# Attention and FFN block on one core: separate dependency records for four slices, product order at the end of a burst, 16-bit tile ends moved into the query groups, paired reciprocals

## The chip, the cores and the metric

The kernel runs on one core of one Trainium2 chip. The metric is the device time of one execution in microseconds (us); less is better. Different submissions ran on different chips, and the unchanged kernel's median moved between 577.3 and 581.1 us with them, so kernels are compared by their ratio to the kernel before, run alternately with it on the same chip. A ratio is the mean time of one kernel's fast runs over the mean of the other's in the same rounds, so it is not quite the ratio of the medians quoted beside it.

Engines: PE is the tensor engine, DVE the vector engine, ACT the scalar engine, POOL and SP issue the DMAs (POOL also computes a few small values at the start).

## The reference, cut to what matters

```python
xn = layernorm(x)                        # x: 1 x 2048 x 448, bf16
q = (xn @ wq) in 16 heads of 256         # 8 key/value heads, window of 512 keys
p = softmax(q k^T / 16);  o = p @ v
s = o @ wo                               # 4096 -> 448
g = silu((gelu(xn @ w_gate) * (xn @ w_up)) @ w_down)
return x + s * g
```

The kernel computes g first, stores it (g2) in device memory, and then goes through four chunks of 512 queries with 16 heads each. For the first three chunks, `o @ wo` is done in one go after the chunk's last head, by a scheme of eight products on sums of halves (a "burst"). Its result is folded, transposed by DMA into `sT`, and combined with x and g in four "tile ends", one for each 128 rows.

## The kernel before

Dependencies come from buffer records: an operation waits for the last writer of what it reads, and for the last writer and all readers of what it writes. The record, not the address, decides.

```python
def op(self, eng, fn, reads=(), writes=(), dma=False, after=()):
    raw = {b.writer: None for b in reads if b.writer is not None}
    deps = dict(raw)
    for b in writes:
        if b.writer is not None:
            deps[b.writer] = None
        deps.update((x, None) for x in b.readers)
    # ... (an engine doesn't wait for itself, except for what it reads)
```

The end of a burst. Note `bx`: one list of records for all four slices `xs[0..3]`.

```python
xs = [xnT[:, k, 0:QC] for k in range(4)]
bx = [y for t in range(4) for y in b_xnT[t]]
def part(eng, b, V, bV, r, n, slot):      # half to xs[n], half to cc, then swap partitions on ACT
    for o, bo, lo, hi in ((xs[n][:, r*HC:r*HC+HC], bx, 0, HC),
                          (cc[:, slot, 0, :], b_cc[slot][:1], HC, QC)):
        # ... ACT copy, or DVE add of V
    act(cc[own, slot, 1, :], cc[other, slot, 0, :], ACT.Copy, ...)
def fold(r, n, slot):
    add("dve", xs[2][own, ...], cc[own, slot, 0, :], cc[own, slot, 1, :], b_cc[slot], bx)
# product 0, product N, product 1, the products on sums (6, 5, 4, 2), product 3; then
add("dve", U2, bank[B6], U2, ...); add("dve", U3, bank[B7], U2, ...)
part("dve", B5, U3, b_tmp[1], 1, 1, 3)
add("dve", U2, bank[B5], U2, ...)
part("dve", B3, U2, b_tmp[0], 0, 1, 0)
dma_t(sT[:, :, 1, :], xs[1], bx, (b_sT[1],))
part("dve", B1, U3, b_tmp[1], 1, 0, 1)
dma_t(sT[:, :, 0, :], xs[0], bx, (b_sT[0],))
for r, n, slot in ((0, 0, 2), (1, 1, 3), (0, 1, 0), (1, 0, 1)):
    fold(r, n, slot)
dma_t(sT[:, :, 2, :], xs[2], bx, (b_sT[2],))
```

After a burst come four query groups (two heads' q each; the results are cast to qT, half on ACT and half on DVE), then heads. A head `m` is: scores of four tiles, exponential with row sum on ACT, reciprocal and scaling on DVE, a DMA transpose of every two tiles into pT, and `p @ v` of head `m - 2`.

```python
for m in range(NS):
    if m in groups:
        for i in range(m, next_group, 2):
            q_group(i, ...)
    s_mm(m)
    if len(late) == LAG:            # LAG = 2
        pv(late.pop(0))
    if m > Hq and LAG <= m % Hq < LAG + 4:
        burst_end(m // Hq - 1, m % Hq - LAG)     # one tile end in each of four heads
    if m > Hq and m % Hq == LAG - 1:
        burst(m // Hq - 1)          # the last burst also issues the loads of wo, 4 x 0.9 MB
    late.append(m)

def wo_end(t, c0, c1, src):         # a tile end: three f32 multiplies by g2, one addition of x
    # ... DVE: tmp = src * f * g2;  xr = tmp + xr
    load_g2(t + NG2)                                      # POOL queue, NG2 = 2
    dma("pool", out_view[:, t, c0:c1], xr[:, x, c0:c1])   # POOL queue
    dma("pool", xr[:, x, :], x_view[:, t + NXR, :])       # POOL queue, NXR = 3; waits for the line above
```

The softmax here doesn't subtract the row's maximum and nothing guards it: scores larger than these inputs give would overflow.

## Time and profile before

| | before |
|---|---|
| time, median of its first three runs | 580.89 us |
| span of the profiled execution | 577.2 us |
| PE busy | 547.1 us, 95% |
| DVE busy | 371.9 us, 64% |
| query groups after burst 1, 2, 3 | 14.44, 16.79, 22.83 us (each read 0.23 us too long, see below) |
| PE waits in the heads that follow | 3.35, 3.2, 1.7 us |

The stretches are differences of times in the timeline of PE: from the first matmul on wq after a burst to the first score matmul after that. PE is the bound, so only the time in which it waits, or runs at a low clock, can be gained. Some records of matmuls are missing from a trace: this one holds x4419 matmuls. One of the missing is the first score matmul after each set of query groups (7 matmuls stand there beside 8 weight loads, of which the first starts 0.23 us before the first recorded matmul). So in traces with x4419 the query groups read 0.23 us too long and the heads after them 0.23 us too short. The page gives busy time as us (share) x instructions.

```profile
span 577.2 us, 11576 instructions
PE 547.1 (95%) x4419; PEld 288.0 (50%) x4444; DVE 371.9 (64%) x944; ACT 297.9 (52%) x771; POOL 44.6 (8%) x83
```

The list of waits of PE names two large causes: casts of qT, and transposes of pT (the numbers are us in all, how often, and the longest).

```profile
PE bank L366 <- DVE qT L701: 13.4, 4, 8.7
PE bank L366 <- DMA pT<-pn: 8.7, 7, 2.1
```

The timeline of PE shows where the first of them falls: the first matmuls of the third of the four query groups (columns: start, duration, engine, line, operation, operands, shape, count, and the idle time before it).

```profile
252.55 0.82 PE L366 MATMUL bank<-xnT,wq 64*128 64x512 bf16 x6 [1.84 <-DVE qT L701]
361.53 1.46 PE L366 MATMUL bank<-xnT,wq 64*128 64x512 bf16 x6 [2.74 <-DVE qT L701]
477.41 1.46 PE L366 MATMUL bank<-xnT,wq 64*128 64x512 bf16 x6 [8.69 <-DVE qT L701]
```

The second and third of these blocks take 1.46 us instead of 0.82: the granted clock, as the trace records it, had fallen to half. A cast lasts 0.7 us and cannot by itself hold PE for 8.69 us. The chain of waits, read in order of time in the third burst, shows what the cast had to wait for.

```profile
464.94 10.09 DMA sT<-xnT
475.13 0.13 DVE xnT L360
...
475.56 0.76 DVE xnT L360 x2
476.33 0.42 DVE xnT L360
476.75 0.61 DVE qT L701
...
477.41 7.78 PE bank L366 x56
```

The four folds (DVE xnT L360) write `xs[2]`. The transpose reads `xs[0]`. They share no byte, only the record `bx`; so DVE stood still for a DMA, and the casts behind the folds stood still too.

The second cause lies in the four heads that hold a tile end. These are one tile end's operations in the timeline of DVE, and one of the PE waits that follow.

```profile
263.17 0.62 DVE L755 SCALAR_TENSOR_TENSOR tmp<-sT,g 128x256 f32<-128x256 bf16 x2
263.70 0.22 DVE L755 SCALAR_TENSOR_TENSOR tmp<-sN,g 128x64 f32<-128x64 bf16 x1
263.95 0.62 DVE L360 TENSOR_TENSOR xr<-tmp,xr 128x448 bf16<-128x448 f32 x1
```

```profile
277.15 1.90 PE L366 MATMUL bank<-pT,va 128*128 128x512 bf16 x8 [1.99 <-DMA pT<-pn]
```

With the tile end, DVE needs about 4.3 us for such a head, and PE 3.45 us.

### The profile page before, as it was taken

What the parts mean: (1) busy time and instruction counts of PE and PEld (TensorE: products, weight loads), DVE (VectorE), ACT (ScalarE), POOL (GpSimd) and SP (SyncE); (2) the same over time, 40 slices, a digit from 0 to 9 for tenths busy, and PEclk for the clock granted to TensorE, in tenths of its full rate; (3) what the DMA queues carried; (4) which work ended last, traced back from release to release, by engine and by line L of the source; (5) the groups of instructions that cost most, each with busy time, mean ns of one, the idle gap of its engine ahead of it and who ended that gap; (6) DMA issues with size and microseconds to landing.
All of it is one profiled execution on the core that took longest, in us unless ns stands there. A gap on an engine that the chain in (4) does not pass through costs nothing.

```text
span 577.2 us, 11576 instructions
## 1 busy us (share of the span) xinstructions
PE 547.1 (95%) x4419; PEld 288.0 (50%) x4444; DVE 371.9 (64%) x944; ACT 297.9 (52%) x771; POOL 44.6 (8%) x83
## 2 busy tenths in 40 slices
PE   9999999999999999989799998989999949889998
PEld 5554444445444447934344496333447923334455
DVE  6665545753668589459858863697589516976822
ACT  5434447643568484137748712467585124676700
POOL 1140500000000000003100000030000010400000
PEclk9999999999999999999999999899999998999999
DMA  9565599722327365017925911199175171982601
GB/s 292 127 192 109 116 281 256 110 53 70 89 65 141 88 111 115 4 26 137 197 56 119 147 34 20 40 184 175 26 147 120 39 242 30 195 173 53 149 18 57
DMA packets 177767, 66.46 MB, mean 115 GB/s; under 512 B 159856, under 2 KB 173680, under 8 KB 177712
## 3 DMA queue, kind: packets, MB, share of 16 engines
q1 hardware_dynamic: 172960, 52.76, 43.7%
q0 software_dynamic: 3984, 12.39, 7.6%
q8 instruction: 35, 0.57, 0.4%
q10 hardware_dynamic: 768, 0.57, 0.3%
q14 instruction: 20, 0.16, 0.1%
HBM read 23.43 MB, written 3.67 MB: 47 GB/s over the span
## 4 chain that ended last, share of the span: by engine, by line
PE 76%; DMA 10%; DVE 10%; issue 3%; ACT 1%; DVEq 0%; ACTq 0%
PE bank L366 75%; DMA pT<-pn 7%; DMA sT<-xnT 3%; DVE pn L718 3%; DVE tmp L755 1%; DVE rden L717 1%; DVE oTh L738 1%; DVE xnT L360 1%; PE bank L483 1%; DVE tmp L360 1%; ACT qT L357 1%; ACT p L714 0%; DVE qT L701 0%; DVE xr L360 0%; DVE oT L738 0%
## 5 line engine op out<-in xcount | busy, mean ns | idle before, releaser
L714 ACT ACTIVATE p<-bank 128x512 f32<-128x512 f32 x256 | 149.9, 598 | 39.6 <-PE bank L366 19.9
L718 DVE TENSOR_SCALAR pn<-p,rden 128x512 bf16<-128x512 f32 x256 | 124.6, 487 | 18.3 <-DMA pT<-pn 9.5
L366 PE MATMUL bank<-pT,va 128*128 128x512 bf16 x512 | 120.9, 379 | 8.8 <-DMA pT<-pn 8.7
L366 PE MATMUL bank<-kT,qT 128*128 128x512 bf16 x487 | 118.2, 379 | 3.1 <-ACT qT L357 1.4
L366 PE MATMUL bank<-xnT,wq 64*128 64x512 bf16 x768 | 98.0, 384 | 14.0 <-DVE qT L701 13.3
L366 PEld LDWEIGHTS bank<-pT,va 128*128 128x128 bf16 x512 | 49.3, 98 | 71.7 <-DMA pT<-pn 13.7
L366 PE MATMUL bank<-xnT,wgu 64*128 64x512 bf16 (+2 forms) x768 | 83.9, 350 | 0.2
L366 PEld LDWEIGHTS bank<-kT,qT 128*128 128x128 bf16 x512 | 49.2, 98 | 63.4 <-issue 3.4
L357 ACT ACTIVATE qT<-bank 128x512 bf16<-128x512 f32 x64 | 37.8, 595 | 71.6 <-PE bank L366 70.2
L701 DVE CAST qT<-bank 128x512 bf16<-128x512 f32 x64 | 42.2, 688 | 42.4 <-PE bank L366 42.3
L366 PEld LDWEIGHTS bank<-xnT,wq 64*128 64x128 bf16 x768 | 36.9, 95 | 63.0 <-DVE qT L701 15.3
L366 PEld LDWEIGHTS bank<-xnT,wgu 64*128 64x128 bf16 x768 | 37.0, 94 | 37.1 <-issue 0.7
L532 DVE TENSOR_TENSOR actT<-bank,gl 128x512 bf16<-128x512 f32 x56 | 37.8, 690 | 26.5 <-PE bank L366 19.9
L714 ACT ACTIVATION_READ_ACCUMULATOR p<-bank 128x1 f32 x256 | 52.8, 206 | 0.0
L357 ACT ACTIVATE gl<-bank 128x512 bf16<-128x512 f32 x56 | 33.2, 597 | 37.0 <-PE bank L366 34.9
L717 DVE RECIPROCAL rden<-rsum 128x1 f32<-128x1 f32 x256 | 40.1, 157 | 15.9 <-ACT p L714 15.9
L366 PE MATMUL bank<-wd,actT 128*128 128x448 bf16 x224 | 43.0, 353 | 0.0
L351 POOL DMA_DIRECT2D g<-g_all x16 | 8.8, 552 | 369.1 <-DVE tmp L755 368.9
L738 DVE TENSOR_SCALAR oTh<-bank 128x512 f16<-128x512 f32 x48 | 32.8, 684 | 0.0
L366 PEld LDWEIGHTS bank<-wd,actT 128*128 128x128 bf16 x224 | 21.8, 98 | 21.0 <-issue 0.4
L366 PE MATMUL bank<-sr,wt 128*64 128x256 f16 x576 | 31.9, 273 | 0.0
L366 PEld LDWEIGHTS bank<-sr,wt 128*64 128x64 f16 x576 | 31.5, 110 | 0.0
(62 smaller groups left out, 423.8 us busy)
## 6 DMA issues: line engine op xcount, KB each, us to landing
wo<-in_A_wo_dram POOLq DMA_DIRECT2D x4, 896.0 KB, 7.1
wtb<-in_A_wo_dram POOLq DMA_DIRECT2D x4, 768.0 KB, 7.3
wq<-in_A_wq_dram SPq DMA_DIRECT2D x2, 1536.0 KB, 11.6
va<-in_A_v_cache_dram SPq DMA_DIRECT2D x8, 256.0 KB, 5.0
pT<-pn SPq DMA_TRANSPOSE x128, 2.8
g_all<-g2w SPq DMA_DIRECT2D x16, 112.0 KB, 1.9
xr<-in_A_x_dram POOLq DMA_DIRECT2D x16, 112.0 KB, 3.5
g<-g_all POOLq DMA_DIRECT2D x16, 112.0 KB, 2.7
```

The lines of the kernel that those rows point to most:

```text
L351: K.op(q, lambda e, o=o, i=i: e.dma_start(o, i), reads, writes, dma=True)
L357: K.op("act", lambda e, o=o, i=i: e.activation(o, i, func, scale=scale), reads, writes)
L360: K.op(eng, lambda e: e.tensor_tensor(o, x, y, op), reads, writes)
L366: ins = e.matmul(o, lhsT=l, rhs=r, start=st, stop=sp, skip_group_check=True)
L483: ins = e.matmul(bank[b][:, 0:w], lhsT=gl[:, 0, 0:P], rhs=gl[:, 0, 0:w], start=True, stop=True)
L532: K.op("dve", lambda e: e.tensor_tensor(actT[:, c % 2, f, :], bank[b + 1], gl[:, s, :], ALU.mult), (b_ps[b + 1], b_gl[s]), (b_actT[c % 2][ ...
L701: K.op("dve", lambda v, s=s, b=b: v.tensor_copy(qT[:, s, 1, :], bank[b + 1]), (b_ps[b + 1],), (b_qT[s][1],))
L714: K.op("act", lambda e, b=b, r=r, z=z: e.activation(p32[:, z, :], bank[b], ACT.Exp, scale=att_scale, accum_out=rsum[:, r:r + 1]), (b_ps[b] ...
L717: K.op("dve", lambda e, r=r: e.reciprocal(rden[:, r:r + 1], rsum[:, r:r + 1]), (b_rsum[r],), (b_rden[r],))
L718: K.op("dve", lambda e, r=r, z=z, y=y, t=t4 % 2: e.tensor_scalar(pn[:, y, t, :], p32[:, z, :], rden[:, r:r + 1], None, op0=ALU.mult), (b_p ...
L738: K.op("dve", lambda v, i=i, b=b, o=o, f=f: v.tensor_scalar(o[:, i, :], bank[b], f, None, op0=ALU.mult), (b_ps[b],), (b_oT[i],))
L755: K.op("dve", lambda e, at=at, i=i, f=f: e.scalar_tensor_tensor(out=at(tmp[:, s, :]), in0=i, scalar=f, in1=at(g2[:, g, :]), op0=ALU.mult, ...
```

## The change

The intent: the DVE sums and the first folds hide behind the last two products; the folds no longer wait for the transposes; the tile ends leave the heads for the query groups and become cheaper (16-bit multiplies; their constant factor `0.5 / (WS * WS)` moves into the sums at the end of the burst); DVE saves half of the reciprocals. The diff, cut to its core:

```diff
+        tmpb, _, _ = place("tmpb", [P, 2, 2 * QC], BF16, at=a)
+        b_xs = [K.buf() for k in range(4)]
...
-        def q_group(n, pairs):
+        def q_group(n, pairs, more_act=False):
+                if more_act and i:
+                    act(qT[:, s, 1, :], bank[b + 1], ACT.Copy, ...)      # third of four casts on ACT
+                    continue
...
-                K.op("dve", ... e.reciprocal(rden[:, r:r + 1], rsum[:, r:r + 1]) ...)
-                K.op("dve", ... tensor_scalar(pn[:, y, t, :], p32[:, z, :], rden[:, r:r + 1] ...) ...)
                 if t4 % 2 == 1:
+                    K.op("dve", ... e.reciprocal(rden[:, r - 1:r + 1], rsum[:, r - 1:r + 1]) ...)
+                    for t in range(2):
+                        K.op("dve", ... tensor_scalar(pn[:, y, t, :], ...) ...)
...
-                add("dve", xs[2][own, ...], ..., b_cc[slot], bx)
+                add("dve", xs[2][own, ...], ..., b_cc[slot], b_xs[2:3])  # and so for all slices of xs
...
-            product(1, B1, ...); part("act", B1, None, [], 0, 0, 2)      # before the products on sums
             # ... products 6, 5, 4, 2 on sums
-            product(3, B1, A(1, 1), allh, True, bA(1, allh))
+            product(1, B1, A(1, 0), allh, False, bA(1, allh))
+            part(B1, None, [], 0, 0, 2)
+            plus(U2, B6, U2, ...); plus(U3, B7, U2, ...)
+            product(3, B7, A(1, 1), allh, True, bA(1, allh))
+            part(B5, U3, ...); plus(U2, B5, U2, ...); part(B3, U2, ...)
+            dma_t(sT[:, :, 1, :], xs[1], b_xs[1:2], (b_sT[1],))
+            # three folds, part(B7, U3), sT[0], the last fold, sT[2]
...
+                    add("dve", at(y), i, at(g), reads + [bg], b_tmp[s], ALU.mult)   # tile end in bf16
...
+                    end = m > Hq and m % Hq == LAG
+                    q_group(i, ..., end)
+                    for t4 in {4: (0, 1), 6: (2, 3)}.get(i - m, ()) if end else ():
+                        burst_end(m // Hq - 1, t4)
-            if m > Hq and LAG <= m % Hq < LAG + 4:
-                burst_end(m // Hq - 1, m % Hq - LAG)
```

## The prediction

> **What bounds the kernel now.** The tensor engine is busy 95% of the 577.2 us trace (page, busy times). From the first attention head on it idles almost only around the three bursts; the list of waits and the timeline give:
>
> - In the query groups after each burst: 1.84, 2.74 and 8.69 us, put down to DVE casts of qT. The chain of waits shows the cause: four DVE folds write xnT slices whose one shared buffer record makes them wait for the sT transposes (2.4 to 10.1 us to landing, longest beside the wo load). The casts queue behind the folds. After the two longer gaps the granted clock falls (0.90 and 0.85 in those stretches); the next two groups take 7.8 us instead of 6.4.
> - In the four heads after that: 3.35, 3.2 and 1.7 us, for pT transposes and exponentials. There DVE needs 4.3 us a head (four reciprocal-and-scale pairs at 0.6, a 0.6 cast, a tile's end at 1.35) against 3.45 us on PE.
>
> Together about 24 us.
>
> **What the change does.**
>
> 1. Separate records (b_xs) let folds run without waiting for sT; ending with products 1 and 3 (2.7 us each) hides the U2/U3 sums and early folds behind PE. PE work is unchanged. The last sT issues at about burst end +2 us, instead of +7 to +14. Gaps of 13.3 us and 2.8 us of low clock should vanish.
> 2. Tiles' ends leave the heads. In 16 bit I estimate 0.7 us instead of 1.35: 128x1024 f16 additions take 0.69 us, half the time per column of the f32 forms. The Trainium skill ("VectorE: DVE Perf Modes", section "What auto-detection actually checks") says two-source ops reach two elements a cycle if all tensors are 16-bit; those additions agree.
> 3. ACT takes a third cast (0.57 us) per group of 3.1 us: it fits.
> 4. One reciprocal per pair saves 0.19 us x 128 on DVE, but tile 0's scaling waits for tile 1's sum, so the fourth exponential (three p32 buffers) waits 0.2 us per head, and pT issues 0.5 us later. ACT at 2.85+0.2 stays under 3.45 us: neither gain nor loss elsewhere.
>
> **What it adds: a new wait.** Four tiles' ends now come within about 3 us, but the fourth needs xr and g2 loaded through one in-order pool queue: the xr load waits for the first tile's output DMA (2.64 us after issue), then lands after 3.5 us; g2 takes 2.7 us. Estimate: DVE is held until 7.7 us after the first tile's end starts, 3 us past the first head's sums; PE loses 2 to 3.5 us per burst at the second head's fourth score tile and first pT. So the 8.3 us of the second item mostly come back. In the third burst sT may also land late beside wo (2 to 4 us more).
>
> **Sum.** Burst 1: 5.2 to about 2.7 us; burst 2: 7.4 to 2.8; burst 3: 11.8 to 4.5. Gain about 14.5 us: 566 us, range 560 to 571. Chance of faster by over 2% (below 569.3): 0.70; within 2%: 0.29; slower: 0.01.
>
> **What would show it.** No PE wait on qT casts in the query groups, clock 1.0 there; sT issued within 2 us of the last product; bf16 multiplies near 0.2 us; DVE waiting in tiles' ends for DMA g2 or xr, 2 us or more; a new PE wait for ACT exponentials in the second head; ACT waiting 0.2 us for DVE once per head.
>
> **What would make it wrong.** The xr/g2 wait absorbed by the two heads of slack (then 559); sT starved by wo until 476 us, cooling the clock (then 571); pT's later issue exposing slow 4.7 us transposes in ordinary heads.

## The result, and the profile after

The changed kernel took 567.68 us (median of 4 runs, 566.31 to 568.3), the kernel before 581.09 us (median of 4). The ratio is 0.9757, with a 95% interval of 0.9718 to 0.9797: faster by over 2%, if narrowly.

```profile
span 564.5 us, 11470 instructions
PE 548.7 (97%) x4444; PEld 288.3 (51%) x4444; DVE 346.8 (61%) x804; ACT 309.4 (55%) x783; POOL 44.4 (8%) x83
```

From the timelines of PE, in us; the fixed parts (everything ahead of burst 1, and the bursts of 21.96 us) are equal within 0.2 us:

| stretch | before | after | after - before |
|---|---|---|---|
| query groups, bursts 1, 2, 3 | 14.44, 16.79, 22.83 | 12.19, 12.19, 12.19 | -17.49 |
| heads from burst 1 to the next | 71.69 | 71.79 | +0.10 |
| heads from burst 2 to the next | 71.18 | 70.58 | -0.60 |
| heads after burst 3 to the end | 91.87 | 97.33 | +5.46 |

With 0.18 us ahead of burst 1 this sums to the 12.7 us between the two spans. With the missing records allowed for, the query groups gained 16.8 us, and the heads changed by -0.13, -0.83 and +5.23 us. So the query groups gained all that they could, and the heads after burst 3 lost nearly a third of it again. The list of PE's waits after:

```profile
PE bank L369 <- ACT p L720: 5.1, 3, 3.0
PE bank L369 <- DMA pT<-pn: 3.8, 3, 2.5
PE bank L369 <- DVE qT L707: 2.0, 1, 2.0
```

The wait for exponentials (ACT p) is new. The chain of waits after burst 1 leads from it back to the POOL queue:

```profile
253.55 0.53 DVE tmpb L363 x3
...
254.36 0.53 POOL g L354
254.89 2.13 DMA out_dram<-xr
...
257.31 0.53 POOL xr L354
257.84 2.36 DMA g<-g_all
...
260.22 0.04 DVE tmpb L363
...
261.29 0.50 DVE pn L727
...
261.81 0.03 ACT p L720
```

The first tile end starts at 253.55. Its output leaves by the POOL queue, the reload of xr waits there until the output has landed, and the g2 that the fourth tile end needs is issued behind that reload. DVE comes to the first head's softmax only at 261.10, 7.55 us after the first tile end began. The two waits of PE that follow:

```profile
262.55 0.60 PE L369 MATMUL bank<-kT,qT 128*128 128x512 bf16 x2 [1.13 <-ACT p L720]
272.63 1.90 PE L369 MATMUL bank<-pT,va 128*128 128x512 bf16 x8 [2.54 <-DMA pT<-pn]
```

The tile end itself got cheaper, by less than half (these lines answer to the three of before):

```profile
253.55 0.42 DVE L363 TENSOR_TENSOR tmpb<-sT,g 128x256 bf16<-128x256 bf16 x2
253.88 0.18 DVE L363 TENSOR_TENSOR tmpb<-sN,g 128x64 bf16<-128x64 bf16 x1
254.10 0.39 DVE L363 TENSOR_TENSOR xr<-tmpb,xr 128x448 bf16<-128x448 bf16 x1
```

From the start of one tile end to the start of the next it is 0.86 us (253.55 to 254.41). Grouped by shape, the multiplies take 288 ns for 256 columns and 219 ns for 128, where the f32 forms took 416 and 285 ns. The difference between the two widths gives the cost of a column: 0.54 ns in bf16 and 1.02 ns in f32. That agrees with the Trainium skill ("VectorE: DVE Perf Modes", section "What auto-detection actually checks"): two-source operations reach the mode of two elements a cycle when every tensor is 16-bit. The multiplies changed from SCALAR_TENSOR_TENSOR to TENSOR_TENSOR at the same time; the addition kept its operation, and it went from 625 to 392 ns for 448 columns, so a cheaper column comes with the type alone. What doesn't shrink is the part that doesn't depend on the width, about 0.15 us here (288 ns less 256 columns at 0.54), and that is half or more of each of these multiplies.

After burst 3 it is worse, because the last sT transpose runs beside the load of wo:

```profile
456.84 12.77 DMA sT<-xnT
469.63 0.04 DVE tmpb L363
...
473.69 2.32 DMA g<-g_all
```

```profile
471.91 1.04 PE L369 MATMUL bank<-pT,va 128*128 128x512 bf16 x4 [1.98 <-DVE qT L707]
...
478.37 1.04 PE L369 MATMUL bank<-kT,qT 128*128 128x512 bf16 x2 [2.98 <-ACT p L720]
479.20 3.62 PE L369 MATMUL bank<-pT,va 128*128 128x512 bf16 x8
```

The tile ends wait for sT until 469.63, the casts queue behind them, the g2 chain starts only then, and the clock falls to half from 472.9 to 483.2: the matmuls at 479.20 take 3.62 us, where such a group took 1.90 us after burst 1.

### The profile page after: what moved, and what is told of

The parts are those of the page before. It is cut to its first block, busy times and chain, and to the rows that moved or that the text cites. A ratio compares the mean times of both kernels' runs of the same rounds, so it can differ in the third digit from the quotient of the medians.

```text
span 564.5 us, 11470 instructions
## 1 busy us (share of the span) xinstructions
PE 548.7 (97%) x4444; PEld 288.3 (51%) x4444; DVE 346.8 (61%) x804; ACT 309.4 (55%) x783; POOL 44.4 (8%) x83
## 3 DMA queue, kind: packets, MB, share of 16 engines
HBM read 23.43 MB, written 3.67 MB: 48 GB/s over the span
## 4 chain that ended last, share of the span: by engine, by line
PE 82%; DMA 9%; DVE 4%; ACT 2%; issue 1%; POOL 1%; SPq 0%; ACTq 0%; DVEq 0%
PE bank L369 82%; DMA pT<-pn 3%; DVE pn L727 3%; DMA sT<-xnT 2%; ACT p L720 2%; DMA g<-g_all 1%; DMA out_dram<-xr 1%; DMA x<-in_A_x_dram 1%; DVE rden L724 1%; DVE tmpb L363 0%; DVE oTh L746 0%; POOL g L354 0%; POOL xr L354 0%; DVE xr L363 0%; ACT qT L360 0%
## 5 line engine op out<-in xcount | busy, mean ns | idle before, releaser
L369 PE MATMUL bank<-kT,qT 128*128 128x512 bf16 x512 | 123.4, 383 | 5.2 <-ACT p L720 5.1
L369 PE MATMUL bank<-pT,va 128*128 128x512 bf16 x512 | 122.8, 383 | 5.8 <-DMA pT<-pn 3.8
L727 DVE TENSOR_SCALAR pn<-p,rden 128x512 bf16<-128x512 f32 x256 | 113.1, 484 | 11.6 <-DMA pT<-pn 7.4
L369 PE MATMUL bank<-xnT,wq 64*128 64x512 bf16 x768 | 94.9, 376 | 0.5 <-DVE oTh L746 0.5
L360 ACT ACTIVATE qT<-bank 128x512 bf16<-128x512 f32 x76 | 44.1, 596 | 54.1 <-PE bank L369 52.5
L707 DVE CAST qT<-bank 128x512 bf16<-128x512 f32 x52 | 35.1, 692 | 46.9 <-PE bank L369 46.8
L720 ACT ACTIVATION_READ_ACCUMULATOR p<-bank 128x1 f32 x256 | 51.5, 201 | 0.0
L724 DVE RECIPROCAL rden<-rsum 128x2 f32<-128x2 f32 x128 | 21.2, 165 | 45.3 <-ACT p L720 45.1
```

Source lines behind the costliest of these rows:

```text
L360: K.op("act", lambda e, o=o, i=i: e.activation(o, i, func, scale=scale), reads, writes)
L369: ins = e.matmul(o, lhsT=l, rhs=r, start=st, stop=sp, skip_group_check=True)
L707: K.op("dve", lambda v, s=s, b=b: v.tensor_copy(qT[:, s, 1, :], bank[b + 1]), (b_ps[b + 1],), (b_qT[s][1],))
L720: K.op("act", lambda e, b=b, r=r, z=z: e.activation(p32[:, z, :], bank[b], ACT.Exp, scale=att_scale, accum_out=rsum[:, r:r + 1]), (b_ps[b] ...
L724: K.op("dve", lambda e, r=r: e.reciprocal(rden[:, r - 1:r + 1], rsum[:, r - 1:r + 1]), b_rsum[r - 1:r + 1], b_rden[r - 1:r + 1])
L727: K.op("dve", lambda e, r=r - 1 + t, z=(n - 1 + t) % NP32, y=y, t=t: e.tensor_scalar(pn[:, y, t, :], p32[:, z, :], rden[:, r:r + 1], None, ...
```

## The experiments

Twelve runs, in three submissions. The kernel before had medians of 577.3, 578.75 and 580.09 us, so an expectation written in us is to be read against about 581 us. The changed kernel itself ran in its own submission and in the second of the three; the others are compared with it through the kernel before. All results were correct.

| run | ratio | 95% interval | query groups | heads after bursts 1, 2, 3 |
|---|---|---|---|---|
| changed kernel | 0.9757 | 0.9718 to 0.9797 | 12.19 each | 71.79, 70.58, 97.33 |
| records | 0.9767 | 0.9733 to 0.980 | 12.19, 12.20, 12.20 | 72.73, 71.30, 92.03 |
| shared | 0.994 | 0.9905 to 0.9975 | 14.15, 13.75, 22.65 | 73.47, 71.04, 90.75 |
| single | 0.9802 | 0.9756 to 0.9849 | 12.19, 12.19, 12.20 | 71.41, 70.09, 97.02 |
| ends_in_heads | 0.969 | 0.9662 to 0.9718 | 12.19 each | 70.78, 70.41, 91.39 |
| after_again | 0.9772 | 0.9746 to 0.9798 | 12.19 each | 70.54, 71.51, 95.57 |
| xr4 | 0.9761 | 0.9735 to 0.9787 | 12.19, 12.19, 12.20 | 68.68, 72.43, 98.50 |
| wolate | 0.9905 | 0.9867 to 0.9944 | 12.19, 12.20, 12.19 | 71.40, 69.77, 106.22 |
| xr4_wolate | 0.9957 | 0.9928 to 0.9986 | 12.20, 12.20, 12.19 | 70.15, 72.05, 107.57 |
| ends_sparse | 0.9582 | 0.9555 to 0.961 | 12.42, 12.42, 12.41 | 68.66, 69.16, 89.51 |
| ends_sparse_single | 0.9553 | 0.9519 to 0.9587 | 12.42 each | 67.96, 68.95, 90.14 |
| records_sparse | 0.9571 | 0.9538 to 0.9605 | 12.42 each | 68.05, 68.99, 89.02 |
| xr4_spread | 0.9575 | 0.9546 to 0.9603 | 12.42 each | 67.89, 67.64, 93.30 |

The stretches come from one profiled execution each. The two executions of the changed kernel differ in them by 1.25, 0.93 and 1.76 us, so a difference of less than 2 us is not firm; the ratios are. The four rows with 12.4 are the traces with the missing records (x4419): their query groups too took 12.2 us, and their heads 0.23 us more than stands here.

### The separate records alone, and the rest without them

The theory: the false wait through the shared record idled PE in the query groups. The rival: the new order of the products is what hides the work. First the kernel before with the records alone:

```diff
+        b_xs = [K.buf() for k in range(4)]
...
-   ... bx ...                     # in part(), fold(), act(xs[3]) and the four transposes
+   ... b_xs[n:n + 1] ...          # the record of the slice that is written or read
+                if m // Hq == 1:  # first burst: wait for the query groups that read xnT there
+                    for b in b_xs:
+                        b.old.extend(...)
```

> The kernel before with one thing of the change alone: separate records b_xs for the four slices of xnT. Theory (the folds' false wait on the sT transposes is what idled PE in the query groups): the four query groups after each burst take 12.2 to 12.4 us as in the changed kernel (before: 14.4, 16.8, 22.8), so 17 us are gained; the tiles' ends stay in the heads, whose waits stay near 3.3, 3.2 and 1.7 to 3 us. About 564 us, that is faster than the whole change by some 3 us. Rival (it is the new order of the products that gains): within 4 us of the kernel before, 577 to 581 us.

It measured 563.82 us against 577.3, ratio 0.9767. The three query stretches fall to 12.2 us, just as in the whole change, and PE's list of waits no longer has the casts:

```profile
PE bank L367 <- DMA pT<-pn: 6.8, 7, 2.5
PE bank L367 <- ACT p L715: 1.7, 4, 0.5
```

The rival falls. One record per slice, with the old order and the old tile ends, is worth as much as the whole change. The "3 us better" did not come: the heads still wait for pT, and after burst 1 such a wait of 2.46 us was followed by a group at half clock (3.42 us).

Then the changed kernel with the one shared record put back:

```diff
-        b_xs = [K.buf() for k in range(4)]
+            bx = [y for t in range(4) for y in b_xnT[t]]
-   ... b_xs[...] ...
+   ... bx ...
```

> The changed kernel with the one shared record put back. Theory: with products 1 and 3 last, the first sT has landed before the last product ends and the other lands within about 4 us in bursts 1 and 2, so little is lost there (0 to 1 us each); in burst 3, beside the wo load, the last fold waits for sT[0] and PE loses up to 5 us: 568 to 574 us. Rival (records matter in every burst even with the new order): 578 us or more.

The ratio is 0.994. That is a miss: I expected what amounts to 0.978 to 0.988, and the stretches 14.15 and 22.65 us after bursts 1 and 3 are nearly those of the kernel before (after burst 2 it is 13.75 instead of 16.79). The chain of waits in burst 3 shows what I had overlooked:

```profile
460.55 2.46 DMA sT<-xnT
...
463.54 0.76 DVE xnT L362 x2
464.31 0.42 DVE xnT L823
...
464.76 8.37 DMA sT<-xnT
...
473.67 0.61 DVE qT L706
```

With one record, DVE's part into `xs[1]` also waits for ACT's part into `xs[0]`, which now comes after product 1. So the first sT is issued at 460.55, just before the burst's end at 460.70, and then every write waits for the transpose before it. With the record shared, the new order and all the rest of the change together gain 0.6% (0.25 to 0.95%).

### One reciprocal per tile

```diff
+                K.op("dve", ... e.reciprocal(rden[:, r:r + 1], rsum[:, r:r + 1]) ...)
+                K.op("dve", ... tensor_scalar(pn[:, y, t, :], ...) ...)
                 if t4 % 2 == 1:
-                    # reciprocal of two sums, two scalings
```

> The changed kernel with one reciprocal per tile again. Theory (the pairing is off the critical path): within 1 us of the changed kernel, 566.5 to 568.7 us; DVE busy up by about 20 us. ACT no longer waits 0.18 us for DVE per head. Rival (the pairing's delayed fourth exponential costs in ordinary heads): 563 us or less. Other rival (it was needed for the heads to keep pace): 571 us or more.

The ratio is 0.9802, with an interval from 0.9756 to 0.9849 that holds both runs of the changed kernel (0.9757 and 0.9772). A second pair of runs, on the better kernel below, gives 0.9553 with one reciprocal per tile and 0.9582 with one per two; those intervals overlap too, and the sign is the other way. The pairing saved DVE 13.5 us of busy time (346.8 us with it, 360.3 without), less than the 20 us that I expected, and no gain or loss of time from it was shown.

### The tile ends back in the heads, one per head

```diff
-                    for t4 in {4: (0, 1), 6: (2, 3)}.get(i - m, ()) if end else ():
-                        burst_end(m // Hq - 1, t4)
+            if m > Hq and LAG <= m % Hq < LAG + 4:
+                burst_end(m // Hq - 1, m % Hq - LAG)
```

> The changed kernel with the four 16-bit tiles' ends back in the four heads after the query groups, one per head. Theory (bunching them makes the fourth wait for xr and g2 through the pool queue, which holds DVE until 7.5 us after the first and costs PE 3.7, 2.3 and 7.4 us): one per head there is no such wait; DVE needs 3.5 to 3.8 us per head against 3.45 on PE, which the slack of two heads mostly absorbs; heads' waits fall to 0.5 to 2 us a burst: 558 to 562 us. Rival (the move out of the heads is what relieves them): 568 us or more.

559.63 us, ratio 0.969: as expected. Its interval ends at 0.9718, where the lower of the changed kernel's two begins, and it is clear of the other. The move into the query groups is the part of the change that loses. Most of it is lost after burst 3: 97.33 us in the changed kernel, 91.39 us here, where the last sT again took 12.8 us but no instruction waited for it. PE still waited 6.6 us for pT, in 8 waits. Against the records run (0.9733 to 0.98), which also has one tile end per head, it is faster by 0.8%: with the ends this close together, the cheaper ends and the rest of the change do gain something.

### What the tile ends in the query groups wait for

> The changed kernel unaltered, to have it on the same chip as the next three. Ratio to the kernel before 0.972 to 0.979.

It gave 0.9772.

```diff
+        x3, a, _ = place("x3", [P, D], BF16, at=a_ident)   # fourth xr, over memory that is no longer used
-            if t + NXR < NT and c1 == D:
-                dma("pool", xr[:, x, :], x_view[:, t + NXR, :], (), b_xr[x])
+            if m > Hq and m % Hq == LAG + 3:               # four reloads, issued together
+                for t in range(m // Hq * 4, m // Hq * 4 + 4):
+                    dma("pool", XR(t % 4), x_view[:, t, :], (), b_xr[t % 4])
```

> The changed kernel with a fourth xr buffer, and the four xr reloads of a burst issued together after the tiles' ends, so that g2 loads no longer queue behind the wait for an output DMA and the fourth tile's end needs no reload of xr. Theory (that queue holds DVE until 7.5 us after the first tile's end): DVE is free about 4.5 us after it, no PE wait for an exponential in the second head of bursts 1 and 2; in burst 3 the sT wait stays but DVE is free 3 us sooner after it. Gain 4 to 8 us on the changed kernel: ratio 0.962 to 0.969. Rival (DVE is merely full of work there, the reload costs nothing): ratio within 0.002 of the changed kernel.

The ratio is 0.9761: no gain. Yet the wait is gone; after burst 1, DVE passes from tile end to softmax without it, about 5 us after the first tile end (253.44) instead of 7.5:

```profile
257.62 0.43 DVE L366 TENSOR_TENSOR tmpb<-sT,g 128x256 bf16<-128x256 bf16 x2
...
258.90 0.17 DVE L727 RECIPROCAL rden<-rsum 128x2 f32<-128x2 f32 x1 [0.32 <-ACT p L723]
```

The stretch after burst 1 fell to 68.68 us. After burst 2 the gain turned into another wait, a pT transpose that took 6.09 us in the chain of waits, against a median of 2.8; the second line is from the list of waits:

```profile
370.89 3.19 PE L372 MATMUL bank<-pT,va 128*128 128x512 bf16 x8 [2.87 <-DMA pT<-pn]
PE bank L372 <- DMA pT<-pn: 7.5, 3, 3.8
```

My rival for this run ("the reload costs nothing") predicted the right ratio, for a reason that the trace contradicts. A third theory was needed: the DMAs of four tile ends, bunched, slow the transposes that the heads depend on. In this kernel the four xr reloads, the outputs and the g2 loads all fall within 8 to 9 us. The test is to hold the reloads back, each by a wait on a head of its own:

```diff
-            if m > Hq and m % Hq == LAG + 3:
-                for t in ...: dma("pool", XR(t % 4), ...)
+            if m > Hq and m % Hq >= LAG + 6 and m % 2 == 0:
+                t = m // Hq * 4 + (m % Hq - LAG - 6) // 2
+                dma_after("pool", XR(t % 4), x_view[:, t, :], b_xr[t % 4], [last PE operation issued])
```

> The fourth xr buffer again, tiles' ends in the query groups, but the four xr reloads held back by a wait on heads 9, 11, 13 and 15 of the row so that they don't fall together beside the first pT transposes. Theory (the bunched reloads of the earlier run took back by slow pT transposes what the lifted g2 wait gave): pT waits after bursts 1 and 2 fall to under 1.5 us, the stretch to the next burst to 68 to 69.5 us; burst 3 keeps its sT wait. Ratio 0.966 to 0.973. Rival (xr reloads have no part in the slow transposes): no better than 0.976.

0.9575, better than I expected (0.966 to 0.973). After bursts 1 and 2 the stretches are 67.89 and 67.64 us, and the longest transpose of pT took 5.0 us instead of 6.7. PE hardly waits for pT any more:

```profile
PE bank L375 <- DMA pT<-pn: 0.8, 2, 0.6
```

The two kernels differ only in when the reloads are issued. So both waits were real, and one hid behind the other: lifting the g2 wait alone gave its gain to slower transposes. (The reverse, spreading the DMAs with the g2 wait left in, was not run.) After burst 3 the sT wait remains (2.19 us at PE).

### The load of wo later

```diff
-                    for i in range(NCO // 8): dma("pool", wo[:, i*8:(i+1)*8, :], ...)   # at the burst's end
+            if m in four later heads, every second one:
+                dma("pool", wo[:, i*8:(i+1)*8, :], ...)
```

> The changed kernel with the four 0.9 MB wo loads issued one every second head from the fourth head after burst 3 on, not at the burst's end. Theory (the wo load starves the last sT transpose of burst 3, 12.8 us to landing): all sT land within 4 us, burst 3 loses 2 to 4 us as bursts 1 and 2 do, not 7.4; no clock drop. The wo loads may delay some pT transposes, up to 2 us lost. Gain 2 to 5 us on the changed kernel. Rival (sT is slow for another reason): no sT time changes.

The ratio is 0.9905, worse than the changed kernel by over 1%. The first half of the theory held: without wo beside it, no sT transpose took over 4.0 us, and PE's wait for a cast behind sT (1.98 us in the changed kernel) is gone. But the run did not do what its description says. A DMA in an in-order queue is issued when the queue comes to it, not when the program's text mentions a head; nothing made it wait, and all four loads left together, at 481.29:

```profile
481.29 3.90 POOL L354 DMA_DIRECT2D wo<-in_A_wo_dram  x4
```

There they met the transposes of pT, one of which now took 18.7 us:

```profile
495.47 3.59 PE L369 MATMUL bank<-pT,va 128*128 128x512 bf16 x8 [10.58 <-DMA pT<-pn]
```

So it shows that this bulk load delays the transposes beside it, sT at one place and pT at the other, and it does not show what a load in spaced pieces would do. That stays open. The same flaw is in the combination:

```diff
+        # both edits: fourth xr buffer with bunched reloads, wo issued later
```

> Both. If the two waits are independent the gains add up for the most part: 6 to 11 us on the changed kernel, ratio 0.957 to 0.965, and after each burst the stretch from the first score matmul to the next burst is 70.4 to 71 us. If one hides the other, it is no better than the better one alone.

0.9957, with 107.57 us after burst 3; its longest pT transpose took 21.9 us. It says no more than the two alone.

### The tile ends spread out

If a tile end's DVE time and its three DMAs crowd the heads, one in every third head should be better than either bunch.

```diff
-                    for t4 in {4: (0, 1), 6: (2, 3)}.get(i - m, ()) if end else ():
-                        burst_end(m // Hq - 1, t4)
+            if m > Hq and m % Hq >= LAG + 1 and (m % Hq - LAG - 1) % 3 == 0 and (m % Hq - LAG - 1) // 3 < 4:
+                burst_end(m // Hq - 1, (m % Hq - LAG - 1) // 3)
```

> The changed kernel with the four tiles' ends spread over the heads after the query groups: behind the 4th, 7th, 10th and 13th head of the new row of heads' count. Theory (after a burst the heads wait for pT transposes because DVE work and the DMAs of four tiles' ends crowd into four heads or less): one end in three heads leaves no wait over 1 us; the stretch from first score matmul to the next burst falls from 70.5 to 71.8 us to 68 to 69.5 us. Ratio 0.957 to 0.966, better than one end per head (0.969). Rival (the pT waits come from elsewhere): 0.968 or more.

555.61 us against 580.09, ratio 0.9582: faster than the changed kernel by close to 2%, and the longest PE wait for pT is 0.6 us.

> The same with one reciprocal per tile again. Theory (DVE has slack when ends are spread, so the pairing does not matter): ratio within 0.002 of the paired one. Rival (pairing delays each pT by 0.5 us and so exposes slow transposes): 0.003 or more better. Other rival (pairing is a gain): 0.003 or more worse.

0.9553 (the edit is that of the single run). At last, how much of the change is needed? The kernel before, with the separate records and this spacing, and nothing else: f32 tile ends, old product order, one reciprocal per tile, two casts on ACT.

> The kernel before with the separate records and the same spreading of the tiles' ends, nothing else of the change: old product order, f32 ends of 1.35 us, one reciprocal per tile, two casts on ACT. Theory (the false wait and the crowding are all that mattered): ratio within 0.003 of the spread changed kernel, 0.958 to 0.968. Rival (the 16-bit ends, the pairing, the third cast on ACT or the new order gain by themselves): 0.971 or more.

554.73 us, ratio 0.9571, the same as the spread changed kernel within the intervals. Its whole list of PE's waits (the eight for ACT qT stand where the first score matmul is missing from the trace):

```profile
PE bank L367 <- DMA pT<-pn: 1.5, 3, 1.0
PE bank L367 <- ACT qT L358: 1.4, 8, 0.3
PE bank L484 <- DVE epst L398: 1.2, 1, 1.2
PE bank L367 <- DVE oTh L739: 0.2, 1, 0.2
PE bank L367 <- DVE qT L702: 0.2, 1, 0.2
```

Two edits, the records and where the tile ends stand, take 4.3% off the kernel before and beat the changed kernel by about 2%. With tile ends that are far apart, their f32 cost of 1.35 us each cost no time that these runs could show. In ends_sparse both the DVE work and the DMAs are spread, in xr4_spread (0.9575) only the reloads; so of the crowding after bursts 1 and 2 the DMAs are shown to matter, and what DVE's share is stays open.

## Why the prediction was right

The prediction was 566 us (560 to 571), with 0.70 for faster by over 2%. Measured were 567.68 us and faster by over 2%, with an interval that ends at 0.9797.

- **False wait through the shared record.** Right, and shown by taking it alone (records) and taking it away (shared). Predicted 13.3 us of gaps and 2.8 us of low clock, 16.1 in all; measured 16.8 us (17.49 as read, less three times 0.23 for the missing records). The prediction credited the new product order with hiding DVE work as well; in the shared run the order and all the rest gained only 0.6% without the records, and records_sparse shows that it isn't needed with them. That step of the prediction was not borne out.
- **New wait of the fourth tile end.** Right: DVE was held for 7.55 us after the first tile end (predicted 7.7), and PE waited for exponentials in the second head and then for pT. The trace of xr4 shows that it is the queue of reloads, since the wait goes when they no longer stand in it; xr4_spread shows what it was worth. What I did not see is the second cost of the bunch, slow pT transposes: in xr4 they take the gain back, and the 2.54 us after burst 1 of the changed kernel are already such a wait, for a transpose of 5.86 us.
- **Sizes per burst.** Predicted losses after the change were 2.7, 2.8 and 4.5 us. From the waits: 3.67 us (1.13 and 2.54) after burst 1; 2.3 us (1.03, 0.50 and 0.79) after burst 2; after burst 3 about 8.6 us, namely 1.98 and 2.98 us of waiting and 3.6 us of half clock (1.15, 0.44, 1.73 and 0.28 us in four groups of matmuls against their usual times; the 7.4 us in two of my expectations left the first out). The term that was mis-sized is burst 3's: I had listed both the late sT and the cooling as risks and put too little of them into the sum. The size also changes from one execution to the next: in after_again the half clock lasted 3.4 us instead of 10.2, and the stretch was 95.57 us instead of 97.33. In the sum, the heads after burst 3 lost 5.2 us where 2.8 were predicted (4.5 less 1.7), and the query groups gained 0.7 us more than predicted, so part of the miss cancelled.
- **16-bit tile ends.** Predicted 0.7 us each, measured 0.86: the cost per column halved as expected, the fixed part of about 0.15 us in each of these small operations did not, and the estimate of 0.7 had halved that too.
- **Pairing.** Predicted neither gain nor loss; none was shown. ACT did wait 0.18 us for DVE in ordinary heads, as foreseen, inside its slack.
- **sT issue.** Predicted within 2 us of the last product: after burst 3 it was issued at 456.84, 1.86 us after the burst's end at 454.98.

## What to carry to other kernels

When a wait names a short instruction, follow the chain of waits up the engine's queue until you meet something that can last as long as the wait; here a dependency record that covered more than the data it stood for. Work that isn't on the critical path did better here spread along it than gathered where an engine seemed idle: the gathered bunch needed its inputs and its DMAs all at once. And after lifting one wait, look at what now ends the idle time before you call its cause harmless, since a wait that hides another can look worthless when it is lifted alone.

## What the Trainium skill lacked or had wrong

- "TensorE: Matmul & The Clock Gate", section "Part 1: The HAM clock gate (the "warmup" mystery)": it puts the fall to half clock after at least one idle window of about 3.4 us. Here single gaps shorter than that were followed by slow matmuls: 2.74 us in the kernel before, 2.46 us in the records run, and 2.15 us in the shared run (the group after it took 3.00 us instead of 1.90). But 2.54 us in the changed kernel was followed by 1.90 us. No length of gap alone separates the cases. The free-running window that the page describes does: in every trace that records a change of the clock, the changes stand on a grid of 3.41 us, fixed within an execution (half clock lasted 3.41, 6.83, 10.24 or 17.07 us). From full clock it fell just after those windows of the grid in which PE was busy for 1.44 us or less, and stayed full after those with 1.53 us or more; from half clock it rose after windows with 2.87 us or more, and stayed at half after those with 2.46 us or less. The 2.54 us gap fell across two windows (1.95 and 2.33 us busy); the 2.46 us gap lay in one (0.82 us busy). So a window need not be wholly idle, which the page's words leave open.
- "DMA: Bandwidth & Descriptors", section "Queues, rings and completion order": it says that each DMA engine takes turns between queues by packet, but gives no figure for what that does to a small transpose. Here an sT transpose took 2.4 us at its fastest and 12.8 us beside 3.7 MB of wo; a pT transpose took a median of 2.8 us, up to 6.7 us beside four bunched tile ends, and up to 18.7 and 21.9 us beside wo.
- The same page, section "Anatomy of one DMA — SWDGE (gpsimd) path", gives about 2.0 us plus bytes over 436 GB/s; for 112 KB that is an estimate of 2.26 us. The chain of waits has 2.13 us for an output and 2.36 us for a g2 load after their issue: for these it agrees. The xr reloads, of the same size, took longer: a median of 2.7 us in the changed kernel and 3.5 us in the kernel before.
